# Attention queries through DRAM, a product that may be put off by a round, and new pacing of the filling work in a two-part kernel

## The chip, the cores and the metric

The kernel runs on one core of one Trainium2 chip. The metric is the device time of one execution in microseconds (us), lower is better. A core has engines that run side by side, each with its own instructions in a fixed order: PE (TensorE, matmuls and their weight loads, PEld), ACT (ScalarE), DVE (VectorE), POOL (GpSimd) and SP (SyncE). POOL, SP and ACT also issue DMAs. Engines wait for each other with semaphores.

## What is computed

Two independent computations whose outputs are put side by side, each 2048 rows x 576 columns:

```python
# A: S4 convolution, D=576 channels, N=128 states, L=2048
dt = exp(log_dt); P = exp(dt*(A_re + 1j*A_im) * l)      # l = 0..2047
K = sum_n(C * P * dt*B).real                            # one filter per channel
y = irfft(rfft(u, 2L) * rfft(K, 2L))[:L] + u * Dskip
# B: attention with 32 heads of 18 columns and one common key and value head
q = x @ wq;  k = x @ wk;  v = x @ wv
p = softmax(q . k * 18**-0.5);  out = (p @ v) @ wo
```

## The kernel before, in words

**The attention is the frame.** The queries lie in 4 chunks c of 512, the heads in 16 pairs pr per chunk, the keys in 16 blocks kb of 128. One step of the main loop's inner unit is one (pair of heads, key block): two score matmuls of PE into one PSUM tile `s` of 128 keys x 1024 (two heads x 512 queries; `scores`, L391, matmuls at L398), one exponential of ACT from `s` into an SBUF tile `P` (`exponentials`, L402, L406), and, for two such units at a time, one product v^T P (`product`, L686): four matmuls side by side at L693 that add into one PSUM tile `ops` over the 16 key blocks. Two pairs of heads, 32 units, make a head group g; 8 groups make a chunk. There are 1024 units.

**Rounds.** The loop at L704 takes NS = 3 units per round: three scores, then three exponentials, and, since one product serves two units, two products in one round and one in the next. There are 342 rounds, the last with one unit. Three PSUM slots hold the scores, so the score of a round waits until the exponential of the same place in the round before has read its slot. NP = 6 tiles hold P, so the exponential of unit i overwrites the tile of unit i - 6, which the product of that unit must have read; `while (i - NP) // 2 >= behind: product(behind)` puts the product ahead of it in the program when it is still missing.

**Fill.** Between the products and behind them, `fill` (L657) puts other work of PE into the round: q (projection of queries, `qproj` L305), op (output projection, L453 and L478), and the convolution's matmuls: kg (filter values, `kgen` L996), hu, lu, hk, lk (transforms, L1039) and iy (back transform). They share one PSUM bank `f`, so that one of them holds it until DVE has read it. All run as generators (`Stream`): the attention's `side` (queries and outputs), `prep` (normalizing), and the convolution's streams.

**The order is fixed at build time.** The programs of PE, ACT and DVE are written in the order in which the Python loop issues them. A small model, `Clock`, holds the time at which PE (`K.t`), DVE (`K.v`) and ACT (`K.a`) would be done, by constants for each operation (a product 0.96, a q group 0.43, an op group 0.50, a kg group 0.75), and the loop fills a round until the next score slot should be free. A credit limits how much fill a round may take; RATE, PACE, AHEAD, TOTAL and LAST (L37 to L41) say how fast the convolution is to move, when it counts as lagging (`lags`, L1190), how far a stream may run ahead and how much fill there is in all. POOL's and SP's orders come from a scheduler.

**Queries.** A unit (c, m) projects the queries of 7 heads (m = 4: of 4 heads) of one chunk. `qproj` leaves them in `f`; DVE or ACT makes qh, a rounded part, and ql, the rest, each in an SBUF tile with a single buffer. `queries` (L341) copies rows of them into the ring `aug`: NAUG = 9 tiles of 128 x 512, each for one pair of heads, a head at rows 0 to 54 and the other at rows 64 to 118 (18 rows qh, 18 qh, 18 ql, one row sh, a bound that is taken off so that the exponential can't overflow). These copies are DMAs from SBUF to SBUF, one per head and part, on POOL's queue (L362; L360 for the first), and one per pair for the row sh (L388). The side stream does not start a unit until the loop is within 56 steps of its due time, and waits in `queries` until the ring's tile is free (a step is two units).

**The convolution.** It runs in 12 chunks of 48 channels. `front(k)`: factors (ACT and DVE), tables (DVE), kg matmuls, the filter to DRAM (kd) and back in another layout (kt). `back(k)`: transforms of u and of the filter, the products of spectra on DVE, iy, and the store.

**The end.** The output projection of the last chunk is partly done in the loop (`outproj_part`, L478), the rest, the last head group included, in `finish` (L502), whose matmuls are named fin.

Of the kernel before, what the change touches and what calls it, by code (L numbers as in the profile page):

```python
# [36 lines left out]
RATE = 1.9  # L37
PACE = 1.8
AHEAD = 0.8
TOTAL = 330.0  # L40
LAST = 500  # L41
NAUG = 9
# [125 lines left out]
class Attention:  # L168
# [36 lines left out]
    def setup(self, tp, conv):  # L205
# [44 lines left out]
        self.aug, self.ready, self.od = {}, set(), {}  # L250
        self.outs, self.step, self.due, self.scaled = [], 0, 1 << 30, {}
        self.o_left = self.q_left = 0
        self.todo, self.busy = [], False
# [31 lines left out]
        while (0, 1) not in self.ready:  # L285
            side.advance()
# [18 lines left out]
    def qproj(self, c, m, xt):  # L305

        nc, V, K = self.nc, self.V, self.k
        m0, mn = MT[m]
        self.q_left = 10
        yield "p", K.fill, False  # L310
        ps = self.bank(CT, f"q{c}_{m}")
        for f in range(2):
            sl = slice(f * 256, f * 256 + 256)
            for k in range(5):
                matmul4(nc, ps[:, sl], self.wq[m][:, k, :], xt[:, k, sl], start=(k == 0), stop=(k == 4))
                K.pe(0.43)
                self.q_left -= 1
                if (f, k) != (1, 4):
# [22 lines left out]
    def queries(self, c, m, qh, ql, ab):  # L341

        nc, V, K = self.nc, self.V, self.k
        m0, mn = MT[m]

        last = 16 * c + ((m0 + mn) // DH - 1) // 2 - NAUG
        while self.step < 16 * (last // 2 + 1):
            yield "w", 0.0, False
        for pr in range(m0 // DH // 2, (m0 + mn) // DH // 2 + 1):
            hs = [h for h in (2 * pr, 2 * pr + 1) if m0 <= h * DH < m0 + mn]  # L350
            if 2 * pr in hs:
                self.aug[(c, pr)] = self.ring[(16 * c + pr) % NAUG]
            for row, src in ((0, qh), (18, qh), (36, ql)):
                for h in hs:
                    r, b = h * DH - m0, 64 * (h % 2) + row

                    q = nc.scalar if (c, m, pr) == (0, 0, 1) and row < 36 else nc.gpsimd
                    t = self.aug[(c, pr)]
                    if q is nc.scalar:
                        q.dma_start(t[b:b + 18, :].bitcast(F32), src[r:r + 18, :].bitcast(F32))  # L360
                    else:
                        q.dma_start(t[b:b + 18, :], src[r:r + 18, :])  # L362
# [19 lines left out]
        V.tensor_scalar(sh, un[0:2, 0:1].broadcast_to([2, CT]), -1.0, None, op0=ALU.mult)  # L382
        for h in range(m0 // DH, (m0 + mn) // DH):
            if h % 2 == 1:
                if (c, m) == (0, 0) and h < 4:
                    (nc.scalar, nc.sync)[h // 2].dma_start(self.aug[(c, h // 2)][54:119:64, :].bitcast(F32), sh.bitcast(F32))
                else:
                    nc.gpsimd.dma_start(self.aug[(c, h // 2)][54:119:64, :], sh)  # L388
                self.ready.add((c, h // 2))

    def scores(self, i, c, pr, kb, cost):  # L391

        nc, K = self.nc, self.k
        t = self.aug[(c, pr)]
        ps = self.ps_s.tile([P, 2, CT], F32, tag="s", name=f"s{c}_{pr}_{kb}")
        for j in range(2):
            r = slice(64 * j, 64 * j + 55)
            nc.tensor.matmul(ps[:, j, :], self.kaug[r, kb * P:(kb + 1) * P], t[r, :], start=True, stop=True)  # L398
        K.pe(cost, K.s[i % NS])
        return ps, K.t + 0.27  # L400
# [52 lines left out]
    def outproj(self, c):  # L453
# [4 lines left out]
        for t in range(4):  # L458
            ob = self.p1.tile([P, D], F32, tag="ob", name=f"ob{c}_{t}")
            for n in range(2):  # L460
                cs = slice(n * 288, (n + 1) * 288)
                ps = self.bank(288, f"op{c}_{t}_{n}")
                for m, (m0, mn) in enumerate(MT):
                    matmul4(nc, ps, o[:mn, m, t * P:(t + 1) * P], self.wo[:mn, m, cs], start=(m == 0), stop=(m == 4))
                    K.pe(0.5)
                    self.o_left -= 1
                    if m < 4:
# [10 lines left out]
    def outproj_part(self, c, ms, part):  # L478
# [4 lines left out]
        for t in range(4):  # L483
            for n in range(2):
# [3 lines left out]
                for m in ms:  # L488
                    matmul4(nc, ps, o[:126, m, t * P:(t + 1) * P], self.wo[:126, m, cs], start=(m == ms[0]), stop=(m == ms[-1]))
                    K.pe(0.5)  # L490
                    self.o_left -= 1
                    if m < ms[-1]:
                        yield "p", 0.0, True
                    self.late.discard((t, n, m))
# [7 lines left out]
    def finish(self, c, part, o_ps, w4, b4):  # L502
# [10 lines left out]
        def begin(t, nh, tile):  # L513

            ps[t, nh] = tile[:, :288]
            for m in range(4):
                if (t, nh, m) in self.late:
                    matmul4(nc, ps[t, nh], o[:126, m, t * P:(t + 1) * P], self.wo[:126, m, cols[nh]], start=(m == min(x[2] for x in self.late if x[:2] == (t, nh))), stop=False)
# [19 lines left out]
        while sums:  # L538
            t, nh = sums.pop(0)
            begin(t, nh, tile[t][:, nh, :])  # L540
            n0, n = n, n + sum(x[:2] == (t, nh) for x in self.late)
# [20 lines left out]
    def side(self):  # L562
# [4 lines left out]
        for c, m in units[1:]:  # L567
            due = 16 * (8 * c + (0, 1, 3, 5, 7)[m])
            self.due = due
            while self.step < due - 56:  # L570
                if self.outs:
                    yield from self.output()
                else:
                    yield "w", 0.0, False
# [3 lines left out]
            for r in self.qproj(c, m, xts[c]):  # L578
                if r[0] == "w" and self.outs:
                    yield from self.output()  # L580
                else:
                    yield r
# [7 lines left out]
    def prepare(self):  # L590

        nc = self.nc
        while True:
# [9 lines left out]
            if c == NCH - 1 and ms[0] == 0:  # L603
                self.part = self.xp.tile([P, 4, D], F32, tag="x", name="part")
                self.late = {(t, n, m) for t in range(4) for n in range(2) for m in range(4)}
# [10 lines left out]
            self.busy = False  # L616

# [17 lines left out]
    def main(self, conv, flag):  # L635
# [16 lines left out]
        def force(done):  # L652
            while not done():
                st = holder()
                (side if st is None else st).advance()

        def fill(then):  # L657
# [3 lines left out]
            while more:  # L661
                more = False
                credit = state["credit"] - (K.t - t - idle)
                urgent = self.due < self.step + 8
                for st in (prep, side, conv) if urgent else (prep, conv, side):
# [3 lines left out]
                    if st.go(self.step, max(credit - 0.3, then - K.t - 0.15, 0.3 * (st is side and side.holds and conv.lags(self.step) and credit > -1.0)), holder()):  # L669
# [10 lines left out]
            if K.t > t:  # L680

                K.t += 0.1
# [3 lines left out]
        def product(n):  # L686
# [8 lines left out]
            K.pe(0.96, done[2 * n + 1] + 0.1, self.o_free if kb == 0 else 0.0)  # L695
            state["credit"] -= 0.96
# [7 lines left out]
        for r in range(0, len(pairs), NS):  # L704
# [3 lines left out]
            for i in new:  # L708
# [3 lines left out]
                force(lambda: (c, 2 * g + j) in self.ready)  # L712
                ss[i] = self.scores(i, c, 2 * g + j, kb, 0.335 if i == r else 0.215)
            K.t += 0.11
# [10 lines left out]
            state["credit"] = min(state["credit"] + NS / 2 * (0.96 + min(max((TOTAL - state["filled"]) / max(LAST - s, 20), 0.45), 0.62 if s < 384 else 0.68)), 0.5 + 0.96)  # L725
# [4 lines left out]
            while behind < r // 2:  # L730
                fill(free() - 0.96 * (r // 2 - behind))
# [4 lines left out]
            nxt = (c, 2 * g + 3) if g < 7 else (c + 1, 1)  # L736
            if kb >= 12 and nxt[0] < NCH:
# [5 lines left out]
        while self.todo or self.busy or holder() or any(m == 0 for _, _, m in self.late):  # L743
# [92 lines left out]
class Conv:  # L836
# [159 lines left out]
    def kgen(self, k, s, ksb):  # L996
        nc, K = self.nc, self.k
        tab = K.v + 0.3
        for q in range(2):
# [9 lines left out]
            K.pe(0.75)  # L1009
# [162 lines left out]
    def go(self, step, credit, lock):  # L1172
        self.turn()
        if self.work > (step + 1) * RATE:
            return False
        for st in self.streams:
# [6 lines left out]
        for st in sorted(self.streams, key=lambda st: (not st.holds, st.work)):  # L1183
            w0 = self.k.work
# [107 lines left out]
```

## Time and profile before

| | us |
|---|---|
| median of 3 runs (lowest, highest) | 1242.33 (1239.46, 1242.68) |
| the profiled execution | 1244.62 |
| its span | 1242.8 |
| first score, last exponential (start) | 33.0, 1222.1 |
| busy: PE, ACT, DVE, POOL | 1157.0, 1045.5, 989.3, 227.6 |
| mean granted clock of TensorE, of full speed | 0.986 |

How to read what follows. A group's row is: line, engine, operation, output<-inputs, tile shapes, number of instructions, then busy time, mean time of one in ns, and the idle time of the engine just before these instructions with what ended most of it. A row of waits is: engine, tile and line <- what it waited for: us in total, times, longest. A timeline's row is: start, length, engine, line, operation, how many instructions are drawn together, and in brackets the idle time before them. Starts and lengths are in us from the start of the span. PE's matmuls overlap in its pipeline, so starts are a better measure than lengths.

### The profile page before, as it was taken

To read this page: it belongs to the slowest core of one execution; us is meant where nothing else is said; L and a number is where in the kernel's file an instruction comes from. 1 tells how busy PE (TensorE), PEld (TensorE's weight loads), DVE (VectorE), ACT (ScalarE), POOL (GpSimd) and SP (SyncE) were. 2 spreads that over 40 slices of the span, in tenths; PEclk is the share of its full clock that TensorE was granted. 3 is DMA by queue.
4 is the path that set the end of the run, shared out by engine and by line. 5 is a ranking of instruction groups with operands and counts; after the bars stand their busy time and mean duration, and the time that the engine had idled before them with its cause. 6 is when DMAs were issued, how large, how long until landed. Compare 5 with 4: busy or idle time off the path is not lost.

```text
span 1242.8 us, 32942 instructions
## 1 busy us (share of the span) xinstructions
PE 1157.0 (93%) x13762; PEld 478.2 (38%) x13762; DVE 989.3 (80%) x1607; ACT 1045.5 (84%) x1101; POOL 227.6 (18%) x451
## 2 busy tenths in 40 slices
PE   5979999899899999999999899899899899999997
PEld 1434244344334344344333343344344334334333
DVE  4656987986995997995997996897896897797753
ACT  2769989989998989888999889888888888888883
POOL 2450320222210210220412200230151110020000
PEclk9989999999999999999999999899999999899999
DMA  7621122113121112122123112112023112012111
GB/s 217 183 52 49 35 73 65 30 37 89 33 86 43 27 32 93 43 58 80 45 62 90 28 39 67 57 36 71 24 49 118 47 37 81 2 36 94 36 40 41
DMA packets 56949, 75.34 MB, mean 61 GB/s; under 512 B 19564, under 2 KB 30188, under 8 KB 56284
## 3 DMA queue, kind: packets, MB, share of 16 engines
q1 hardware_dynamic: 35788, 58.22, 14.5%
q0 software_dynamic: 20320, 14.40, 5.3%
q8 instruction: 110, 1.80, 0.6%
q10 hardware_dynamic: 688, 0.57, 0.2%
q14 instruction: 43, 0.35, 0.1%
HBM read 35.28 MB, written 22.54 MB: 47 GB/s over the span
## 4 chain that ended last, share of the span: by engine, by line
PE 64%; DVE 15%; ACT 11%; issue 4%; DMA 4%; POOL 0%; SPq 0%; ACTq 0%; DVEq 0%
PE ops L693 26%; PE s L398 18%; ACT P L406 10%; PE q L165 5%; PE op L165 4%; DVE tab L95 3%; PE kg L1007 3%; PE iy L165 2%; DVE acc L95 2%; DVE ks L95 2%; DMA xr<-xT 2%; DMA aug<-qh 2%; DVE pt L95 1%; PE hu L165 1%; PE hk L165 1%
## 5 line engine op out<-in xcount | busy, mean ns | idle before, releaser
L406 ACT ACTIVATE P<-s 128x1024 f32<-128x1024 f32 x1024 | 967.7, 1032 | 161.2 <-PE s L398 143.9
L693 PE MATMUL ops<-P,v_sb 128*32 128x512 f32 x4096 | 542.1, 603 | 7.8 <-DVE o L99 7.8
L398 PE MATMUL s<-aug,kaug 55*128 55x512 f32 x2048 | 366.3, 443 | 32.8 <-ACT P L406 30.3
L398 PEld LDWEIGHTS s<-aug,kaug 55*128 55x128 f32 x2048 | 171.2, 185 | 345.6 <-ACT P L406 307.5
L362 POOL DMA_DIRECT2D aug<-qh x252 | 126.2, 509 | 598.1 <-DVE qh L99 323.7
L693 PEld LDWEIGHTS ops<-P,v_sb 128*32 128x32 f32 x4096 | 112.2, 110 | 121.6 <-issue 78.4
L165 PE MATMUL q<-x,wq_sb 128*32 128x256 f32 (+2 forms) x1480 | 107.7, 405 | 5.2 <-DVE sck L95 3.7
L388 POOL DMA_DIRECT2D aug<-sh x62 | 35.2, 574 | 272.6 <-DVE sh L103 271.5
L165 PE MATMUL op<-wo_sb,oT 126*32 126x288 f32 (+1 forms) x1112 | 81.4, 409 | 3.2 <-DVE sck L95 1.9
L165 PEld LDWEIGHTS q<-x,wq_sb 128*32 128x32 f32 (+1 forms) x1480 | 48.9, 112 | 65.0 <-issue 38.8
L362 POOL DMA_DIRECT2D aug<-ql x128 | 63.8, 504 | 6.1 <-DMA aug<-qh 3.7
L95 DVE TENSOR_TENSOR tab<-tab,tt 128x576 f32<-128x576 f32 (+1 forms) x72 | 59.2, 822 | 1.6
L99 DVE COPY ksb<-kg 128x192 f32<-128x192 f32 x48 | 17.5, 365 | 53.3 <-PE kg L1007 52.8
L95 DVE TENSOR_TENSOR tab<-tab 128x576 f32<-128x576 f32 (+1 forms) x72 | 59.0, 820 | 1.0
L95 DVE TENSOR_TENSOR tab<-sum,r 128x576 f32<-128x576 f32 (+1 forms) x72 | 58.9, 818 | 0.0
L95 DVE TENSOR_TENSOR tab<-r,dif 128x576 f32<-128x576 f32 (+1 forms) x72 | 58.8, 817 | 0.0
L95 DVE TENSOR_TENSOR tt<-f,sum 128x576 f32<-128x576 f32 (+1 forms) x72 | 58.8, 817 | 0.0
L165 PEld LDWEIGHTS op<-wo_sb,oT 126*32 126x32 f32 (+1 forms) x1112 | 33.6, 110 | 53.5 <-issue 25.6
L1007 PEld LDWEIGHTS kg<-tab 128*32 128x32 f32 x2304 | 37.4, 112 | 32.0 <-issue 17.2
L1007 PE MATMUL kg<-tab 128*32 128x64 f32 x2304 | 42.6, 223 | 6.9 <-DVE ab L107 5.7
L95 DVE TENSOR_TENSOR acc<-acc,pt 128x1728 f32<-128x1728 f32 (+2 forms) x36 | 48.6, 1350 | 0.2
L95 DVE TENSOR_TENSOR pt<-us,ks 128x1728 f32<-128x1728 f32 (+2 forms) x36 | 48.6, 1351 | 0.0
(121 smaller groups left out, 987.1 us busy)
## 6 DMA issues: line engine op xcount, KB each, us to landing
aug<-qh POOLq DMA_DIRECT2D x252, 36.0 KB, 1.9
od<-o SPq DMA_DIRECT2D x31, 256.0 KB
aug<-ql POOLq DMA_DIRECT2D x128, 36.0 KB, 2.0
u<-u SPq DMA_DIRECT2D x12, 384.0 KB
kd<-ksb SPq DMA_DIRECT2D x12, 384.0 KB
kt<-kd SPq DMA_DIRECT2D x48, 96.0 KB
outa<-u SPq DMA_DIRECT2D x12, 384.0 KB
oT<-od SPq DMA_DIRECT2D x16, 252.0 KB
```

The source lines that it names most:

```text
L95: return self.v.tensor_tensor(out, *a, **k)
L99: return self.v.tensor_copy(out, *a, **k)
L165: nc.tensor.matmul(ps[j:e], w[:, j:e], x, start=start, stop=stop, tile_position=(0, j))
L362: q.dma_start(t[b:b + 18, :], src[r:r + 18, :])
L388: nc.gpsimd.dma_start(self.aug[(c, h // 2)][54:119:64, :], sh)
L398: nc.tensor.matmul(ps[:, j, :], self.kaug[r, kb * P:(kb + 1) * P], t[r, :], start=True, stop=True)
L406: nc.scalar.activation(pt, ps, AF.Exp, scale=SCALE)
L693: nc.tensor.matmul(o_ps[32 * j:32 * j + 32, :], self.v[:, kb, :], pts[2 * n + j // 2][:, j % 2, :], start=(kb == 0), stop=(kb == 15), tile ...
L1007: nc.tensor.matmul(ps[32 * g:32 * g + 32, d, :], t[:, :32], t[:, 32:], start=(j == 0), stop=(j == 1), tile_position=(0, 32 * g))
```

## The change

- **Queries through DRAM.** `queries` writes the parts of all heads of a unit to a DRAM tile qd of the chunk (three DMAs and one for sh, on POOL's queue); only the first two pairs still go straight into the ring. A new `fetch`, on SP's queue, reads each pair from there into a ring of 6 tiles in place of 9 (two DMAs of 55 x 512 per pair), as soon as the tile's former group is over and the queries are there.
- **Queries at any time.** The side stream no longer waits for a due time or for the ring; outputs in the queue go first, then the next unit. `late` says when the side stream may use more than its credit.
- **A product may be put off.** If the last product of a round would end more than DEFER = 0.5 after the next score slot comes free, by the model, the loop leaves it, and it comes in the next round behind the three scores, ahead of the exponential that overwrites its P tile.
- **The convolution's streams** may run further ahead of the model when they lag (up to 1.0 more), and are stopped only when they are 20 ahead.
- **Constants** of the model and of pacing, and the limits of the credit.

```diff
-RATE = 1.9
-PACE = 1.8
-AHEAD = 0.8
-TOTAL = 330.0
+RATE = 1.75
+PACE = 1.68
+AHEAD = 0.7
+TOTAL = 340.0
 LAST = 500
-NAUG = 9
+DEFER = 0.5
+NAUG = 6
+HEAD = 12
+LEFT = 0.85
...
+        self.aug = {n: self.ring[n % NAUG] for n in range(64)}
...
-                K.pe(0.43)
+                K.pe(0.465)
...
-        last = 16 * c + ((m0 + mn) // DH - 1) // 2 - NAUG
-        while self.step < 16 * (last // 2 + 1):
-            yield "w", 0.0, False
-        for pr in range(m0 // DH // 2, (m0 + mn) // DH // 2 + 1):
...
+        n0 = 4 if (c, m) == (0, 0) else 0
+        for h in range(n0):
+            t = self.aug[h // 2]
...
+        for row, src in ((0, qh), (18, qh), (36, ql)):
+            nc.gpsimd.dma_start(qd[h0 + n0:h1, row:row + 18, :], src[n0 * DH:mn, :].bitcast(F32))
...
-        sh = self.p2.tile([2, CT], F32R, tag="sh", name=f"sh{c}_{m}", bufs=1)
+        sh = self.p2.tile([8, CT], F32R, tag="sh", name=f"sh{c}_{m}", bufs=1)
...
+        nc.gpsimd.dma_start(qd[h0 + n0:h1, 54, :], sh[:h1 - h0 - n0, :].bitcast(F32))
+        self.queried = c * H + h1
+
+    def fetch(self, group):
+
+        while self.next < min(64, 2 * group + NAUG) and 2 * self.next + 2 <= self.queried:
+            c, pr = divmod(self.next, 16)
+            t = self.aug[self.next]
+            for j in range(2):
+                self.nc.sync.dma_start(t[64 * j:64 * j + 55, :].bitcast(F32), self.qd[c][2 * pr + j])
+            self.ready.add(self.next)
+            self.next += 1
...
-                    K.pe(0.5)
+                    K.pe(0.485)
...
-            while self.step < due - 56:
-                if self.outs:
-                    yield from self.output()
-                else:
-                    yield "w", 0.0, False
+            while self.outs:
+                yield from self.output()
...
+    def late(self):
+
+        s = self.step
+        if self.due < 128 and self.due - s < 2 * self.q_left + 14:
+            return True
+        return (90, 180, 270, 302)[s // 128] - self.units > LEFT * (128 * (s // 128) + (120, 120, 120, 116)[s // 128] - s)
...
-                    if st.go(self.step, max(credit - 0.3, then - K.t - 0.15, 0.3 * (st is side and side.holds and conv.lags(self.step) and credit > -1.0)), holder()):
+                    spare = credit - 0.3 if st is not side or urgent or late or side.holds else 0.0
+                    wait = then - K.t - (1.2 if st is side and not urgent and not side.holds and self.units > 0.64 * self.step + HEAD else 0.15)
+                    if st.go(self.step, max(spare, wait, 0.3 * (st is side and side.holds and conv.lags(self.step) and credit > -1.0)), holder()):
...
-                K.t += 0.1
+                K.t += 0.03
...
-            K.pe(0.96, done[2 * n + 1] + 0.1, self.o_free if kb == 0 else 0.0)
-            state["credit"] -= 0.96
+            K.pe(0.88, done[2 * n + 1] + 0.1, self.o_free if kb == 0 else 0.0)
+            state["credit"] -= 0.88
...
-            K.t += 0.11
+            K.t += 0.22
...
-            state["credit"] = min(state["credit"] + NS / 2 * (0.96 + min(max((TOTAL - state["filled"]) / max(LAST - s, 20), 0.45), 0.62 if s < 384 else 0.68)), 0.5 + 0.96)
+            state["credit"] = min(state["credit"] + NS / 2 * (0.88 + min(max((TOTAL - state["filled"]) / max(LAST - s, 20), 0.45), 0.7 if s < 384 else 0.9)), 1.2 + 0.88)
...
             while behind < r // 2:
-                fill(free() - 0.96 * (r // 2 - behind))
+                fill(free() - 0.88 * (r // 2 - behind))
+
+                if behind == r // 2 - 1 and K.t + 0.88 > free() + DEFER:
+                    break
                 product(behind)
                 behind += 1
             fill(free())
             c, g, kb, j = pairs[new[-1]]
-            nxt = (c, 2 * g + 3) if g < 7 else (c + 1, 1)
-            if kb >= 12 and nxt[0] < NCH:
+            self.group = (new[-1] + 1) // 32
+            self.fetch(self.group)
+            nxt = 16 * c + 2 * g + 3
+            if kb >= 12 and nxt < 64:
                 force(lambda: nxt in self.ready)
...
-            K.pe(0.75)
+            K.pe(0.665)
...
-        if self.work > (step + 1) * RATE:
+        lag = step * RATE - self.work
+        if lag < -20.0:
             return False
+        ahead = AHEAD + min(max(lag, 0.0) / 20.0, 1.0)
...
-            w0 = self.k.work
+            w0, st.ahead = self.k.work, ahead
```

More of the change, by code (lines that the diff above doesn't have):

```diff
@@ L249, in setup @@
         self.ubound, self.first = None, True
-        self.aug, self.ready, self.od = {}, set(), {}
+        self.aug = {n: self.ring[n % NAUG] for n in range(64)}
+        self.ready, self.od, self.qd = set(), {}, {}
+        self.next, self.queried = 2, 0
         self.outs, self.step, self.due, self.scaled = [], 0, 1 << 30, {}
-        self.o_left = self.q_left = 0
-        self.todo, self.busy = [], False
+        self.o_left = self.q_left = self.units = 0
+        self.todo, self.busy, self.group = [], False, 0
         conv.begin()
@@ L344, in queries @@
         m0, mn = MT[m]
[L346 to L362 removed]
+        h0, h1 = m0 // DH, (m0 + mn) // DH
+        if m == 0:
+            self.qd[c] = self.dr.tile([H, 55, CT], F32, tag="qd", name=f"qd{c}")
+        qd = self.qd[c]
+        n0 = 4 if (c, m) == (0, 0) else 0
+        for h in range(n0):
+            t = self.aug[h // 2]
+            for row, src in ((0, qh), (18, qh), (36, ql)):
+                b = 64 * (h % 2) + row
+                q = nc.scalar if h // 2 == 1 and row < 36 else nc.gpsimd
+                q.dma_start(t[b:b + 18, :].bitcast(F32), src[h * DH:h * DH + DH, :].bitcast(F32))
+        for row, src in ((0, qh), (18, qh), (36, ql)):
+            nc.gpsimd.dma_start(qd[h0 + n0:h1, row:row + 18, :], src[n0 * DH:mn, :].bitcast(F32))
         self.first = False
@@ L380, in queries @@
         self.ubound = un
-        sh = self.p2.tile([2, CT], F32R, tag="sh", name=f"sh{c}_{m}", bufs=1)
[L382 to L389, printed above, removed]
+        sh = self.p2.tile([8, CT], F32R, tag="sh", name=f"sh{c}_{m}", bufs=1)
+        V.tensor_scalar(sh, un[0:8, 0:1].broadcast_to([8, CT]), -1.0, None, op0=ALU.mult)
+        for pr in range(n0 // 2):
+            (nc.scalar, nc.sync)[pr].dma_start(self.aug[pr][54:119:64, :].bitcast(F32), sh[0:2, :].bitcast(F32))
+            self.ready.add(pr)
+        nc.gpsimd.dma_start(qd[h0 + n0:h1, 54, :], sh[:h1 - h0 - n0, :].bitcast(F32))
[8 more added lines that the diff above has]
+            self.next += 1
     def scores(self, i, c, pr, kb, cost):
         nc, K = self.nc, self.k
-        t = self.aug[(c, pr)]
+        t = self.aug[16 * c + pr]
         ps = self.ps_s.tile([P, 2, CT], F32, tag="s", name=f"s{c}_{pr}_{kb}")
@@ L516, in begin @@
             for m in range(4):
-                if (t, nh, m) in self.late:
-                    matmul4(nc, ps[t, nh], o[:126, m, t * P:(t + 1) * P], self.wo[:126, m, cols[nh]], start=(m == min(x[2] for x in self.late if x[:2] == (t, nh))), stop=False)
+                if (t, nh, m) in self.rest:
+                    matmul4(nc, ps[t, nh], o[:126, m, t * P:(t + 1) * P], self.wo[:126, m, cols[nh]], start=(m == min(x[2] for x in self.rest if x[:2] == (t, nh))), stop=False)
         def end(t, nh):
@@ L540, in finish @@
             begin(t, nh, tile[t][:, nh, :])
-            n0, n = n, n + sum(x[:2] == (t, nh) for x in self.late)
+            n0, n = n, n + sum(x[:2] == (t, nh) for x in self.rest)
             if n0 < 5 <= n:
@@ L577, in side @@
                 yield "v", self.k.t + 6.0, False
[L578 to L582, printed above, removed]
+            yield from self.qproj(c, m, xts[c])
         self.due = 1 << 30
@@ L604, in prepare @@
                 self.part = self.xp.tile([P, 4, D], F32, tag="x", name="part")
-                self.late = {(t, n, m) for t in range(4) for n in range(2) for m in range(4)}
+                self.rest = {(t, n, m) for t in range(4) for n in range(2) for m in range(4)}
             if ms[0] == 3:
@@ L735, in main @@
             c, g, kb, j = pairs[new[-1]]
-            nxt = (c, 2 * g + 3) if g < 7 else (c + 1, 1)
-            if kb >= 12 and nxt[0] < NCH:
+            self.group = (new[-1] + 1) // 32
+            self.fetch(self.group)
+            nxt = 16 * c + 2 * g + 3
+            if kb >= 12 and nxt < 64:
                 force(lambda: nxt in self.ready)
@@ L741, in main @@
             behind += 1
-        while self.todo or self.busy or holder() or any(m == 0 for _, _, m in self.late):
+        while self.todo or self.busy or holder() or any(m == 0 for _, _, m in self.rest):
             if self.todo or self.busy:
```

16 lines of the change are left out of this document (9 added, 7 removed).

## The prediction, made before the changed kernel ran

> **What bounds the kernel now.** I read the busy times and groups of the page first, then the waits, then short timelines in steady, crowded and stalled stretches.
>
> ```profile
> PE 1157.0 (93%) x13762; PEld 478.2 (38%) x13762; DVE 989.3 (80%) x1607; ACT 1045.5 (84%) x1101; POOL 227.6 (18%) x451
> PE 64%; DVE 15%; ACT 11%; issue 4%; DMA 4%; POOL 0%; SPq 0%; ACTq 0%; DVEq 0%
> L406 ACT ACTIVATE P<-s 128x1024 f32<-128x1024 f32 x1024 | 967.7, 1032 | 161.2 <-PE s L398 143.9
> L693 PE MATMUL ops<-P,v_sb 128*32 128x512 f32 x4096 | 542.1, 603 | 7.8 <-DVE o L99 7.8
> L398 PE MATMUL s<-aug,kaug 55*128 55x512 f32 x2048 | 366.3, 443 | 32.8 <-ACT P L406 30.3
> ```
> ```profile
> PEld s L398 <- ACT P L406: 307.5, 445, 1.5
> ACT P L406 <- PE s L398: 143.9, 224, 8.2
> DVE qh L99 <- DMA aug<-sh: 12.0, 1, 12.0
> ACT P L406 <- PE ops L693: 7.7, 5, 4.0
> PE kg L1007 <- DVE ab L107: 5.7, 1, 5.7
> ```
>
> PE and ACT wait for each other in turn: PE's score for a free score slot (445 times), ACT's exponential for a score (224 times, 143.9 us in all). So a round of three scores and three exponentials is as long as the slower of the two, and a change in their coupling moves the end directly. An exponential waits for a *product* only 5 times. How long a round is, two timelines show (start, length, engine, instruction, idle before):
>
> ```profile
> 139.90 5.61 ACT L406 ACTIVATE P<-s 128x1024 f32<-128x1024 f32 x6 [0.19 <-PE s L398]
> 141.89 0.49 PE L398 MATMUL s<-aug,kaug 55*128 55x512 f32 x2 [0.20 <-ACT P L406]
> 142.81 0.49 PE L398 MATMUL s<-aug,kaug 55*128 55x512 f32 x2 [0.42 <-ACT P L406]
> 143.23 1.92 PE L693 MATMUL ops<-P,v_sb 128*32 128x512 f32 x16
> 145.08 0.97 PE L398 MATMUL s<-aug,kaug 55*128 55x512 f32 x6
> 145.68 5.61 ACT L406 ACTIVATE P<-s 128x1024 f32<-128x1024 f32 x6 [0.18 <-PE s L398]
> ```
> ```profile
> 198.05 5.61 ACT L406 ACTIVATE P<-s 128x1024 f32<-128x1024 f32 x6 [0.66 <-PE s L398]
> 201.38 1.06 PE L693 MATMUL ops<-P,v_sb 128*32 128x512 f32 x8
> 202.27 0.83 PE L165 MATMUL hk<-kt,dft_sb 128*32 128x192 f32 x16
> 202.91 1.04 PE L693 MATMUL ops<-P,v_sb 128*32 128x512 f32 x8
> 203.89 0.96 PE L398 MATMUL s<-aug,kaug 55*128 55x512 f32 x6
> 204.49 2.85 ACT L406 ACTIVATE P<-s 128x1024 f32<-128x1024 f32 x3 [0.84 <-PE s L398]
> 204.78 0.86 PE L165 MATMUL lk<-kt,dft_sb 128*32 128x192 f32 x16
> ```
>
> Exponentials that follow each other start 0.91 apart ((2.85 - 1.03)/2), a round of three takes ACT 2.73. A product adds 1.92 - 1.06 = 0.86 to PE, the hk fill 202.91 - 202.27 = 0.64, and three scores that wait for nothing 204.78 - 203.89 = 0.89, with change-over about 1.0. Call W the products and fills of a round. Where the third score had to wait for ACT, everything behind it is late, and the round takes 1.33 + W: in the first fence six exponentials and the gap take 145.68 - 139.90 = 5.78 = 2.73 + 3.05, and 1.33 + 2 x 0.86 = 3.05; in the second 6.44 = 2.73 + 3.71, and 1.33 + 0.86 + 0.64 + 0.86 = 3.69. So the rule is max(2.73, 1.33 + W) behind a wait, else max(2.73, 1.0 + W). Over the 341 rounds of the order before it adds to 1149. The trace has 1221.46 - 33.03 = 1188.4 (first score to the last round's), so some 39 us are stalls, about 10 of them in the head, the rest places such as these:
>
> ```profile
> 33.03 1.95 PE L398 MATMUL s<-aug,kaug 55*128 55x512 f32 x6 [1.70 <-DMA aug<-qh]
> 66.51 0.69 DVE L99 CAST qh<-q 126x512 fp32r<-126x512 f32 x1 [12.04 <-DMA aug<-sh]
> 68.67 1.51 PE L1007 MATMUL kg<-tab 128*32 128x64 f32 x48 [5.67 <-DVE ab L107]
> 72.71 1.02 ACT L406 ACTIVATE P<-s 128x1024 f32<-128x1024 f32 x1 [8.19 <-PE s L398]
> 971.03 1.02 ACT L406 ACTIVATE P<-s 128x1024 f32<-128x1024 f32 x1 [3.96 <-PE ops L693]
> 1221.46 0.51 PE L398 MATMUL s<-aug,kaug 55*128 55x512 f32 x2
> 1224.13 2.61 PE L165 MATMUL fin<-wo_sb,oT 126*32 126x288 f32 x40
> ```
>
> **The change, part by part.** *Queries through DRAM.* POOL's small copies into the ring go, SP gets 124 more transfers.
>
> ```profile
> L362 POOL DMA_DIRECT2D aug<-qh x252 | 126.2, 509 | 598.1 <-DVE qh L99 323.7
> L388 POOL DMA_DIRECT2D aug<-sh x62 | 35.2, 574 | 272.6 <-DVE sh L103 271.5
> aug<-qh POOLq DMA_DIRECT2D x252, 36.0 KB, 1.9
> 47.90 5.12 SPq L303 DMA_DIRECT2D wo_sb<-wo  x5
> ```
> ```profile
> 60.00:65.00 5.00, 3.00 (x30) 0.78 (x18) 0.00 (x0) 4.17 (x5) 3.35 (x7) 1.00 0.69 171
> 65.00:70.00 5.00, 1.33 (x52) 1.36 (x56) 1.98 (x3) 0.00 (x0) 3.77 (x9) 0.73 0.18 38
> ```
>
> POOL's 442 issues (252 + 62 and 128 for ql) become some 70. POOL is busy 18%, so this alone gives nothing; but the single qh buffer came free only when POOL had issued its copies, and in the head that held DVE for 12.04, behind it PE's kernel generation for 5.67, and so ACT for 8.19. With four issues in place of some twenty the buffer is free at once: I take 8 off, between 5.67 (PE's wait alone) and 8.19 + 1.70. What is late next there are the products and fills of those rounds, which the rule above has already. On SP a fetch stands where its ring slot is free, two head groups (21 rounds of at least 2.73, 57 us) ahead of its use; behind it on SP stand loads and stores of the convolution and of the output, which wait with it. The first fetch is another matter: it stands behind the five wo loads (47.90, 5.12 long), the windows (last but one column: busy share of the DMA engines) show the transfers at 0.69 from 60 to 65 and at 0.18 behind it, and it is wanted at round 11, 33.03 + 11 x 2.73 = 63 at the earliest. Cost 0 to 3; I take 0, since fills make those rounds longer than 2.73. The sh tile has 8 rows in place of 2 and the same 512 columns, so DVE's part is as long as before. The Trainium skill, DMA: Bandwidth & Descriptors (Anatomy of one DMA — SWDGE (gpsimd) path), gives a transfer some 2 us that no size removes, mostly the receipt of the write, heaviest where it lands in HBM; the row has 1.9 for SBUF. By it the two hops in series would be an estimated 4 us or more against 1.9, which speaks against the detour; it stays behind the 57 us.
>
> *Queries at any time, new constants, longer credit.* PE's work in all stays as it is; it lies in other rounds. By the rule without any new wait the order of the changed kernel adds to 1135 in place of 1149: -14, nearly all in the last quarter, where fills now stand in rounds that had room. The middle stalls (29 of the 39) come where DVE is behind, as at 971.03; the built order spreads the convolution more evenly, and PE's longer rounds (below) give DVE time. I take -14 of them, between 0 and -29.
>
> *A product put off a round.* This decides. The changed order, read product by product, has the last product of 135 rounds behind the three scores of the next round. The six P buffers stay, so each exponential overwrites the buffer of the exponential six before it, and must wait for the product that reads that one. Before, in 170 rounds the third exponential wants the product of its own round, which by then is done. After, in 85 rounds the *second* wants the product that was put off, in 50 the *first*. Queued behind that exponential are the other exponentials of the round, and behind their ends the next scores. One place of the trace before shows such a wait:
>
> ```profile
> 82.48 1.92 PE L693 MATMUL ops<-P,v_sb 128*32 128x512 f32 x16 [0.32 <-DVE o L99]
> 83.64 1.02 ACT L406 ACTIVATE P<-s 128x1024 f32<-128x1024 f32 x1 [0.20 <-PE ops L693]
> ```
>
> From a product's start to the exponential that it releases are 83.64 - 82.48 = 1.16. Let T be the end of the last exponential of the round before. The third score can go at T + 0.18 (it needs that slot; 0.20 in the row at 141.89), the product 0.42 behind (143.23 - 142.81), the release is T + 1.76. The second exponential wants T + 0.91: stall 0.85. The first wants T: stall 1.76. So these rounds take at least 2.73 + 0.85 = 3.58 and 2.73 + 1.76 = 4.49, whatever PE has to do. Hidden is what PE's own work takes anyway: 1.0 + W is on average 3.1 in the 85 rounds (over 3.58 in 12 of them) and 3.4 in the 50 (over 4.49 in 9). Against the rule without the wait that leaves 0.36 in each of 85 = 31 and 0.84 in each of 50 = 42. And in some 80 rounds behind them PE, which now waited, starts late by 0.33: 27. Together 31 + 42 + 27 - 14 (above) = +86. Carried round by round with the same numbers, so that slack passes on, it is +79; I take +82. Bounds: -14 (all hidden) and 85 x 0.85 + 50 x 1.76 + 27 - 14 = +173 (nothing hidden); I stand near the values with the rows' own cover.
>
> *Tail.* Six more groups of the output projection are left behind the last product: five take 2.61 (1224.13), one 0.5, so +3; PE is alone there.
>
> Sum, against the profiled execution: 1244.6 + 82 - 8 - 14 + 3 = 1307.6. It stands 2.3 above the median of the runs, 1242.3, so the forecast is **1305**.
>
> **The rivals.** *The wait on P is hidden.* If the put-off product nearly always stands in rounds in which PE is the late one, the exponential comes late with or without it. For it: 224 waits of ACT for scores. Against: with six buffers and a first exponential that needs the product, the product stands between two things that ACT needs; putting it off brings the scores early and the exponentials no earlier. It decides where PE's own work passes 3.58 or 4.49, which 21 of the 135 do by my count. Then 1242.3 - 14 - 8 + 3 = 1223, with the middle stalls as they are: **faster**, or 1209 with them gone.
>
> *Fetches come late.* SP issues in order; a fetch that stands behind a store that waits for DVE reaches its pair too late. Each group of the 30 would then hold the scores for, say, the 1.9 of a landing twice: 30 x 3.8 = 114 on top, some 1400 with all of them, 1345 with a third. Against: 57 us of lead.
>
> *The change does not do what it says*: the product is hardly ever put off. The built order, with 135 such rounds, excludes it for the order itself; the effect is then that of the first rival.
>
> **How the numbers follow.** My forecast, waits on P in 135 rounds: 0.80, over 1263 (half of the +82 hidden, 1305 - 41) to 1342 (0.27 more in each of the 135 rounds, since the 1.16 is read at one place: +37). Hidden: 0.12, of which 0.11 ends below 1238.6 and 0.01 between. Late fetches: 0.08, above 1342. The range 1263 to 1342 leaves out 0.20. About 0.3% is what a measurement of this kernel can tell from no change: faster 0.11, same 0.01, slower 0.88.
>
> **What would show it.** Right: the waits of exponentials for products rise from 7.7 us, 5 times, to some 90 us in over 100; the 12.04 of DVE for qh and the 8.19 of ACT near 72 go; POOL's issues fall to some 70; no score waits for a transfer beyond the first round. Wrong: exponentials wait for scores as before and hardly for products (first rival); scores wait for fetches (second); ACT's gaps near 72 stay, or the idle time of the tail grows by more than 3.

## The result

The changed kernel takes 1323.02 us (median of 6 runs, 1317.89 to 1323.46), the kernel before 1240.78 (6 runs, 1239.46 to 1242.68): ratio 1.0648, 95% interval 1.0626 to 1.067. It is slower, by 82 us where 63 were forecast, and inside the range.

The page of the changed kernel, the lines that answer to those shown of before (busy times; the chain by engine; the groups of exponentials, products and scores, whose lines are now L417, L708 and L409):

```profile
PE 1199.6 (91%) x13762; PEld 481.7 (36%) x13762; DVE 988.8 (75%) x1601; ACT 1050.3 (80%) x1101; POOL 57.0 (4%) x97
PE 62%; ACT 19%; issue 8%; DVE 8%; DMA 2%; POOL 0%; ACTq 0%; SPq 0%; DVEq 0%
L417 ACT ACTIVATE P<-s 128x1024 f32<-128x1024 f32 x1024 | 972.3, 1030 | 231.2 <-PE ops L708 137.5
L708 PE MATMUL ops<-P,v_sb 128*32 128x512 f32 x4096 | 532.5, 609 | 5.9 <-DVE o L103 5.9
L409 PE MATMUL s<-aug,kaug 55*128 55x512 f32 x2048 | 405.9, 461 | 75.2 <-ACT P L417 65.0
```

The exponentials have not become longer (1030 ns on average in place of 1032), and their number is the same. ACT's idle time before the exponentials went from 161.2 to 231.2, and what ends it is another engine's other instruction: before it was the scores (143.9), now it is the products (137.5). In the chain of work that ended last ACT went from 11% to 19%. Of the 43 us that PE is busy longer, 40 are in the scores (405.9 against 366.3), which are the same matmuls. The waits of the changed kernel (us, times, longest):

```profile
PEld s L409 <- ACT P L417: 331.8, 557, 1.7
ACT P L417 <- PE ops L708: 137.5, 136, 3.1
ACT P L417 <- PE s L409: 88.9, 119, 10.3
```

The built order has 135 rounds in which a first or second exponential reads behind a product. In 130 of them the trace has the wait, 49 times at the first exponential (82.8 us) and 81 times at the second (51.8); the other 6 of the 136 waits are at third exponentials. Before there were 5, all at third ones. Two of the waits in a row, in the timeline (a product is eight matmul records):

```profile
58.78 1.36 PE L409 MATMUL s<-aug,kaug 55*128 55x512 f32 x6
60.07 1.92 PE L708 MATMUL ops<-P,v_sb 128*32 128x512 f32 x16
61.23 3.77 ACT L417 ACTIVATE P<-s 128x1024 f32<-128x1024 f32 x4 [1.64 <-PE ops L708]
62.78 0.94 PE L409 MATMUL s<-aug,kaug 55*128 55x512 f32 x4
64.14 0.50 PE L409 MATMUL s<-aug,kaug 55*128 55x512 f32 x2 [0.41 <-ACT P L417]
64.56 1.06 PE L708 MATMUL ops<-P,v_sb 128*32 128x512 f32 x8
65.72 2.86 ACT L417 ACTIVATE P<-s 128x1024 f32<-128x1024 f32 x3 [0.72 <-PE ops L708]
```

The three scores start at 58.78; ACT, idle from 59.59, waits 1.64 until the put-off product (60.07) has read the P tile that the first exponential overwrites: 61.23 - 60.07 = 1.16. At 64.14 the third score waits for its slot, the product follows 0.42 behind, and 65.72 - 64.56 is 1.16 again: the second exponential is 0.72 late. Over all rounds of either kind the median from the product's start to the exponential is 1.16 too.

Where the time lies, from the starts of the exponentials of rounds 0, 10, 85, 171, 256 and 341 in the traces (us between them, then their sum):

```
                          0-10   10-85  85-171  171-256  256-341    loop
before                    41.8   252.5   297.9    298.8    296.9  1187.9
changed                   37.9   276.9   322.9    322.0    301.3  1261.0
changed, 8 tiles for P    38.3   264.5   297.8    296.6    282.6  1179.8
changed, never put off    35.0   260.7   309.7    305.2    293.7  1204.3
detour alone              33.6   254.1   299.3    303.2    296.6  1186.9
```

The first exponential starts at 36.1 in place of 34.2, and what follows the last one takes 3.1 more: 1.9 + 73.1 + 3.1 = 78.1 = 1320.9 - 1242.8, the difference of the spans. The 1.9 at the start differs from run to run: with 8 tiles for P the first exponential starts at 33.9.

### The profile page after: what moved, and what is told of

Its sections match the earlier page's. It is cut to its first block, busy times and chain, and to the rows that moved or that the text cites. A ratio compares the mean times of both kernels' runs of the same rounds, so it can differ in the third digit from the quotient of the medians.

```text
span 1320.9 us, 32516 instructions
## 1 busy us (share of the span) xinstructions
PE 1199.6 (91%) x13762; PEld 481.7 (36%) x13762; DVE 988.8 (75%) x1601; ACT 1050.3 (80%) x1101; POOL 57.0 (4%) x97
## 4 chain that ended last, share of the span: by engine, by line
PE 62%; ACT 19%; issue 8%; DVE 8%; DMA 2%; POOL 0%; ACTq 0%; SPq 0%; DVEq 0%
PE ops L708 29%; ACT P L417 18%; PE s L409 18%; PE op L169 4%; PE q L169 3%; PE kg L1027 2%; PE iy L169 2%; DVE ks L99 1%; DMA xr<-xT 1%; PE hu L169 1%; DVE tab L99 1%; PE fin L169 1%; PE lk L169 1%; PE hk L169 1%; DVE sck L99 1%
## 5 line engine op out<-in xcount | busy, mean ns | idle before, releaser
L417 ACT ACTIVATE P<-s 128x1024 f32<-128x1024 f32 x1024 | 972.3, 1030 | 231.2 <-PE ops L708 137.5
L708 PE MATMUL ops<-P,v_sb 128*32 128x512 f32 x4096 | 532.5, 609 | 5.9 <-DVE o L103 5.9
L409 PE MATMUL s<-aug,kaug 55*128 55x512 f32 x2048 | 405.9, 461 | 75.2 <-ACT P L417 65.0
L409 PEld LDWEIGHTS s<-aug,kaug 55*128 55x128 f32 x2048 | 175.2, 186 | 389.8 <-ACT P L417 331.8
L708 PEld LDWEIGHTS ops<-P,v_sb 128*32 128x32 f32 x4096 | 103.6, 110 | 162.5 <-issue 136.6
L169 PE MATMUL q<-x,wq_sb 128*32 128x256 f32 (+2 forms) x1480 | 104.0, 394 | 1.3 <-DVE sck L99 1.2
L99 DVE TENSOR_TENSOR sck<-lk,sck 128x384 f32<-128x384 f32 x48 | 24.5, 552 | 44.2 <-PE lk L169 44.2
L103 DVE COPY o<-ops 128x512 f32<-128x512 f32 x31 | 21.4, 689 | 36.5 <-PE ops L708 34.4
L365 POOL DMA_DIRECT2D qd<-qh x40 | 25.3, 637 | 507.6 <-DVE qh L103 507.6
```

The lines of the kernel that those rows point to most:

```text
L99: return self.v.tensor_tensor(out, *a, **k)
L103: return self.v.tensor_copy(out, *a, **k)
L169: nc.tensor.matmul(ps[j:e], w[:, j:e], x, start=start, stop=stop, tile_position=(0, j))
L365: nc.gpsimd.dma_start(qd[h0 + n0:h1, row:row + 18, :], src[n0 * DH:mn, :].bitcast(F32))
L417: nc.scalar.activation(pt, ps, AF.Exp, scale=SCALE)
L708: nc.tensor.matmul(o_ps[32 * j:32 * j + 32, :], self.v[:, kb, :], pts[2 * n + j // 2][:, j % 2, :], start=(kb == 0), stop=(kb == 15), tile ...
```

## The experiments

Theory A: the time is lost because an exponential overwrites a P tile that the put-off product, now in its own round, has still to read. Rivals: B, the detour through DRAM and the new pacing cost the time; C, the fetches come late; D, the price belongs to the reuse of the tile and not to the place of the product.

**Never put off.**

```diff
-DEFER = 0.5
+DEFER = 1e9
```

> The changed kernel, but no product is ever put off (DEFER so large that the test never holds); its built order has 170 rounds whose third exponential reads behind a product of its own round, as before, and none with a wait of the first or second. Theory A (the put-off product holds the exponentials, the P tile being reused): the round rule adds to 1162 over the order of this kernel, the stalls of the kernels so far are 24 to 39, start and tail 59: 1245 to 1260, exponentials wait for products under 10 us. Rival B (DRAM detour and new pacing cost the time, the putting off is harmless or helps): 1310 or more, ACT's waits for scores above 150 us.

Measured: 1265.67, ratio to before 1.0189 (1.0171 to 1.0207). Exponentials wait for products 8.4 us in all, and for scores 160.7:

```profile
L417 ACT ACTIVATE P<-s 128x1024 f32<-128x1024 f32 x1024 | 966.7, 1034 | 180.1 <-PE s L409 160.7 <-DMA kaug<-keys 9.9 <-PE ops L708 8.4
```

57 of the 82 us are gone with the putting off, so B in its strong form falls. But the time is 6 above A's range: with products where they were before, the other edits cost 24. The wait for scores, 160.7 where B asked for over 150, fits that: part of the loss is B's.

**More tiles for P.** PE, ACT and DVE run the same operations in the same order as the changed kernel; only the memory behind P is larger, with the semaphore waits that follow from it, and a ring of 5 in place of 6 makes the room.

```diff
-NAUG = 6
+NAUG = 5
...
-        self.pp = ctx.enter_context(self.tc.tile_pool(name="a_p", bufs=NP))
+        self.pp = ctx.enter_context(self.tc.tile_pool(name="a_p", bufs=8))
```

> The changed kernel with 8 tiles for P in place of 6, the rule that forces a product into the program left at 6, and the ring of queries 5 tiles in place of 6 to make room: the programs of PE, ACT and DVE are the same instruction for instruction, only SP's fetches move. No exponential then wants a product that stands in its own round, but for the third in 50 rounds. Theory A: the rule without the wait adds to 1135, with 24 to 39 of stalls and 59 of start and tail 1218 to 1233: faster than before. Rival B (pacing, detour): within 10 of 1323. Rival C (fetches are late): slower than 1323, since a fetch has one group less of lead.

Measured: 1239.58, ratio 0.9972 (0.9955 to 0.999). The waits of this kernel:

```profile
PEld s L409 <- ACT P L417: 242.3, 409, 1.7
ACT P L417 <- PE s L409: 150.8, 205, 8.5
PE s L409 <- ACT P L417: 20.3, 62, 0.4
ACT P L417 <- PE ops L708: 1.5, 2, 1.1
```

The wait of 137.5 is 1.5, and 83 us are gone, without one operation moved on the three engines. This settles A: the loss is the reuse of the P tiles. C falls too: the fetches have less lead here (in the trace each pair has landed 11.6 us or more ahead of its first score, 13.8 in the changed kernel), and nothing waits for them. Against the never-put-off kernel it is 26 us faster, so under the new pacing putting off seems to be worth something where it waits for nothing; that kernel had 6 tiles and 8.4 us of waits for products, and was not run with 8. It misses A's range by 7 on the slow side: the gain that was forecast beside the wait did not come (below).

**7 tiles for P**, the ring of 6, again the same programs: `bufs=7`.

> The changed kernel with 7 tiles for P, all programs the same, the ring of 6 as well. The 50 rounds with a wait of the first exponential become rounds with a wait of the second, the 85 with a wait of the second become ones with a wait of the third, which costs nothing. Theory A: at most 50 x 0.85 = 43 and some late starts behind them above the kernel with 8 tiles, less what is hidden: 1240 to 1270, and exponentials wait for products some 50 times with a median of 0.7. Rivals B and C: 1323.

Measured: 1244.18, ratio 1.0006 (0.999 to 1.0022).

```profile
ACT P L417 <- PE s L409: 117.0, 190, 3.4
ACT P L417 <- PE ops L708: 26.5, 47, 1.9
```

One tile more turns 136 waits into 47 of 0.56 on average (the median is 0.44, where 0.7 was expected), all at second exponentials, and its loop is 3.9 longer (1183.7) than that of 8 tiles. So here the wait of a second exponential is paid for almost wholly by the shorter wait for scores behind it (117.0 against 142.3, which is 150.8 less 8.5 ahead of the very first exponential). That the wait of the first is what costs in the changed kernel follows only if its 85 rounds behave alike, which was not tested.

**The putting off alone, in the kernel before.**

```diff
+DEFER = 0.5
...
                 fill(free() - 0.96 * (r // 2 - behind))
+                if behind == r // 2 - 1 and K.t + 0.96 > free() + DEFER:
+                    break
                 product(behind)
```

> The kernel before, with one part of the change alone: a product may be put off (the test with its own model cost 0.96). Its built order has 108 rounds with a wait of the second exponential and 74 with a wait of the first. Theory A: the rule with the wait adds to 1259 in place of 1149, so with start, tail and stalls as before 1340 to 1355; exponentials wait for products some 180 times, 180 to 210 us idle. Rival B: 1200 to 1245, the waits hidden, since scores come earlier.

Measured: 1447.72, ratio 1.1656 (1.1623 to 1.1688): far outside what either theory expected. The wait is there, and the loop is 1275.5, 87.6 longer:

```profile
ACT P L407 <- PE ops L694: 186.3, 172, 3.0
```

The other 114 us come behind the loop. The last score starts at 1304.0, and then this is left (windows: PE, PEld, DVE, ACT and POOL busy, TensorE's clock, DMA share, GB/s; below them one row of PE's timeline):

```profile
1304.00:1330.00 26.00, 6.81 (x62) 1.93 (x58) 23.91 (x37) 6.67 (x6) 0.00 (x0) 0.70 0.00 1
1330.00:1360.00 30.00, 8.20 (x160) 5.57 (x160) 25.11 (x38) 0.00 (x0) 0.00 (x0) 0.50 0.00 1
1360.00:1390.00 30.00, 12.64 (x204) 6.53 (x200) 17.46 (x28) 0.00 (x0) 0.00 (x0) 0.50 0.12 40
1390.00:1420.00 30.00, 6.67 (x80) 3.33 (x79) 24.75 (x31) 0.00 (x0) 0.00 (x0) 0.50 0.00 0
```
```profile
1347.09 1.51 PE L1010 MATMUL kg<-tab 128*32 128x64 f32 x48 [33.48 <-DVE tab L96]
```

DVE still makes the tables of a convolution chunk after the attention is over. With the old pacing and the putting off the convolution does not get its share of the loop, and its rest runs alone, bound by DVE. Why was not taken apart. In the changed kernel what follows the last exponential is 3.1 longer than before and not 114; that it is the new pacing that prevents it is likely, but no run shows it by itself.

**The detour alone, in the kernel before**: `queries`, `fetch`, the ring of 6 and the calls of `fetch` as in the change; due times, constants and credit as before.

> The kernel before with one part of the change alone: the queries go through DRAM and the ring of 6 (POOL's writes, SP's fetches, no wait for the ring); due times, constants, credit as before, no product put off. Its built order adds by the round rule to 1154 in place of 1149, three groups of the output projection fewer at the end (-1.5). Theory A (the detour costs nothing in the loop, and the wait of DVE for the qh buffer in the head goes): 1233 to 1246. Rival C (the detour holds up SP's queue or the fetches): above 1255, with scores or products waiting for transfers.

Measured: 1245.85, ratio 1.0033 (1.0021 to 1.0044). Rounds 0 to 10 take 33.6 in place of 41.8: the head's wait is gone, 8.2 as the prediction said. The first exponential starts 2.2 later, and from round 10 the loop loses 7.2, of which the order (other rounds are fuller, 1154 in place of 1149 by the round rule) accounts for 5. Nothing in the loop waits for a fetch. So the detour by itself is worth nothing here, and costs 0.3%.

**The put-off product behind the second score.**

```diff
+                if i == r + 2 and behind < (r - NS) // 2:
+                    product(behind)
+                    behind += 1
                 ss[i] = self.scores(i, c, 2 * g + j, kb, 0.335 if i == r else 0.215)
```

> The changed kernel with 6 tiles for P as it is, but a product that was put off stands behind the second score of the next round in place of the third. The built order has 34 rounds in which the first exponential reads behind it and 70 in which the second does. Theory A (the price is the place: the product need not wait for the third score's slot, so it starts 0.91 earlier and releases at T + 0.8 or so in place of T + 1.76): the wait of the second exponential is gone, that of the first falls to some 0.7, 34 x 0.7 = 24 us at most in about 34 waits, total 1240 to 1265. Rival D (the price belongs to the reuse of the tile, wherever the product stands): 34 x 1.64 + 70 x 0.73 = 107 us of waits in 104 places, total 1295 to 1320.

Measured: 1271.73, ratio 1.0226 (1.0207 to 1.0245), between the two. The row of the exponentials, and two places of its timeline:

```profile
L417 ACT ACTIVATE P<-s 128x1024 f32<-128x1024 f32 x1024 | 971.1, 1033 | 184.2 <-PE s L409 115.4 <-PE ops L708 67.7
```
```profile
55.59 1.50 PE L169 MATMUL q<-x,wq_sb 128*32 128x256 f32 x24
57.03 0.73 PE L409 MATMUL s<-aug,kaug 55*128 55x512 f32 x4
57.69 1.07 PE L708 MATMUL ops<-P,v_sb 128*32 128x512 f32 x8
58.85 3.77 ACT L417 ACTIVATE P<-s 128x1024 f32<-128x1024 f32 x4 [1.57 <-PE ops L708]
60.00 1.05 PE L169 MATMUL q<-x,wq_sb 128*32 128x256 f32 x16
60.97 0.73 PE L409 MATMUL s<-aug,kaug 55*128 55x512 f32 x4
61.63 1.07 PE L708 MATMUL ops<-P,v_sb 128*32 128x512 f32 x8
62.80 1.94 ACT L417 ACTIVATE P<-s 128x1024 f32<-128x1024 f32 x2 [0.17 <-PE ops L708]
```

The second exponential's wait falls from 0.72 to 0.17, as the place would have it; the first's is still 1.57 there. PE comes to these scores straight from its fills (q from 55.59, the scores at 57.03 without a wait for a slot), so it is PE and not the slot that sets when the product starts, and standing ahead of the third score helps little. Over all rounds it is alike: 43 waits at second exponentials are 8.1 us, 34 at first ones 52.4. So A holds for the second exponentials and D for the first; both are too simple. How much of the 51 us gained against the changed kernel is the place's is open, since this order also has fewer such rounds (104 in place of 135).

**Versions that keep the putting off and take the wait away.** The rule that forces products set to 8 as well (`NP = 8`, `NAUG = 5`):

> The changed kernel with 8 tiles for P, the ring of 5, and the rule that forces a product set to 8 as well, so that a product that was put off may stand behind the fills of its round. Round rule 1131 in place of 1135, three groups fewer at the end than the kernel with 8 tiles. Theory A: 1230 to 1240, no exponential waits for a product. Rival: the forced place kept PE busy at the right time, 1245 or more.

Measured: 1238.88, ratio 0.9974 (0.9958 to 0.9991), inside A's range, but not told apart from the 1239.58 with the rule at 6. Exponentials still wait for products 3 times, 5.3 us. Then with `LEFT = 0.6`:

> The changed kernel with 8 tiles for P, the rule at 8, the ring of 5, and LEFT = 0.6 in place of 0.85, so that the side stream may exceed its credit earlier. The built order has 7 rounds with over 4.2 us of products and fills (8 with LEFT at 0.85), 4 rounds in which the one bank of the fills changes hands more than once (9), and two groups of the output projection fewer at the end (-1). If the stalls that are left come where fills hand the bank over behind DVE, 1228 to 1237, below the 1238.88 with LEFT at 0.85; if they have nothing to do with the order of the fills, 1237 to 1241.

Measured: 1233.98, ratio 0.9934 (0.9914 to 0.9954): the fastest, 0.66% below the kernel before and 89 us below the changed one. The time fits the forecast that stalls fall with fewer hand-overs of the bank, but the traces do not bear it out: in the profiled executions (1237.65 and 1238.2) exponentials wait for scores 152.2 us, with LEFT at 0.85 they wait 145.4, and the loop is 2.7 longer. What makes it faster stays open.

## Why the prediction was right, and where its sizes were off

The step that decided was right in place, kind and nearly in count: of the 135 rounds forecast 130 show the wait; the price's parts, 0.42 and 1.16, are the same in the changed kernel's timeline; with the tiles free the wait goes and 83 us with it. The idle time is larger than forecast, 137.5 us in place of some 90.

Its size splits into classes when the changed kernel and the one with 8 tiles, which run the same programs, are set side by side (ACT's time between the starts of exponentials above 0.91, added over the rounds of a class, a round going from the last exponential of the round before to its own last):

```
rounds that wait with the   count   forecast   measured
first exponential              50        +42      +72.6
second exponential             85        +31      +18.3
neither (late starts)         205        +27       -9.7
sum                                     +100      +81.2
```

The sum is firm: 81 where 96 (82 + 14) was forecast. Which of the three terms was mis-sized can't be read from it, since the split depends on where a round is cut: from first score to first score, as the prediction's rule counts, the same two traces give +19.9, +48.7 and +13.2.

What is seen directly is this. Ahead of the first exponential of the 50 rounds ACT is idle 1.69 on average (84.4 us), where I had 1.76. PE is not late there: in 44 of the 50 rounds the first score starts more than 0.4 before the last exponential of the round before has ended. So the wait is not hidden in its own round, as I had it for half of it. What it hides is the lateness of the next round: 48 of the 50 are followed by a round in which the second exponential waits, and in these the time ahead of the first exponentials, above 0.91 each, adds to 44.5 with 8 tiles and to 5.1 in the changed kernel. The wait of the second exponentials puts 40.5 in its place.

That the total lies inside the range is in part luck: the wait came out 15 below its forecast, and the terms beside it, together -33 by the forecast (-8, -14 of stalls, -14 of the order, +3), came out at -3, 30 above.

The terms beside it came out worse:

- The last quarter gains 14.3 with 8 tiles (282.6 against 296.9): the -14 that the order's rule had there.
- The head gives 3.5 to 3.9 (rounds 0 to 10), not 8. The wait of DVE for qh is gone, in place of 12.04 stands a wait for the projection itself, 7.5. The detour alone gave 8.2; with the rest of the change q groups fill those early rounds, and in the changed kernel exponentials wait for products in them. The first exponential starts 1.9 later.
- The middle stalls do not go. Rounds 10 to 85 take 12.0 *more* with 8 tiles, though by the rule they should be even. Its trace has seven waits of exponentials above 1.5 us there, 14.7 in all, where the kernel before has two, 4.0 in all; the shorter ones add to the same (18.4 and 18.5). The longest of the seven, in that kernel's timeline:

```profile
227.89 1.07 PE L708 MATMUL ops<-P,v_sb 128*32 128x512 f32 x8
228.88 1.45 DVE L99 TENSOR_TENSOR r<-r,m 128x1248 f32<-128x1248 f32 x1
230.25 0.68 DVE L103 COPY o<-ops 128x512 f32<-128x512 f32 x1
230.98 1.93 PE L708 MATMUL ops<-P,v_sb 128*32 128x512 f32 x8 [2.02 <-DVE o L103]
233.75 1.94 ACT L417 ACTIVATE P<-s 128x1024 f32<-128x1024 f32 x2 [3.59 <-PE s L409]
```

The head group ends at 228.9; the copy of its result, which frees the PSUM tile for the next, stands on DVE behind an operation of the convolution, and PE idles 2.02, and ACT 3.59. Another of the seven (2.45, ending at 318.68) has PE waiting for DVE too; ahead of three (82.53, 185.43 and 261.50; 5.35 in all) PE has no wait but is full of q and products, and ahead of one (207.00, 1.61) it waits for the transfer kt<-kd. I had reasoned that DVE's spare time would absorb the stalls. At two of these places the order of DVE's queue counts, at three how the fills lie. -14 was forecast, +9.7 measured (all rounds from 10 to 256).
- The tail: 3.1, forecast 3.
- POOL's issues fall from 442 to 88, forecast some 70: four for each of 20 units, and 8 straight into the ring.

Together, against the span: +81.2, -14.3, -3.5, +9.7, +1.9 and +3.1 are 78.1.

The first rival (the wait is hidden) is out by the wait's 137.5; so is "the change does not do what it says". The second (late fetches) is out: beyond the first score (3.6, put down to a DRAM write of the head) no score waits for a transfer. Its prices were added loosely: 1305 + 114 is 1419, and with a third 1343, where the prediction has some 1400 and 1345. The queries' way through DRAM takes 5.1 us from issue to landing for the first hop and 2.4 (median, 1.8 to 2.7) for the second. The first pair fetched has only 13.8 from landing to use, not 57 of lead, which is still enough:

```profile
aug<-qd SPq DMA_DIRECT2D x124, 110.0 KB
qd<-qh POOLq DMA_DIRECT2D x30, 252.0 KB, 5.1
qd<-sh POOLq DMA_DIRECT2D x15, 14.0 KB, 1.9
```

The Trainium skill, DMA: Bandwidth & Descriptors (Anatomy of one DMA — SWDGE (gpsimd) path), has a fixed part of some 2 us per transfer, heaviest for writes to HBM. The trace agrees with the 2 us, but does not show that DRAM is the heavier target: 14 KB of sh land there in 1.9, as 36 KB did in SBUF before, and the 5.1 belongs to 252 KB.

## What to carry to other kernels

When work is moved later, look up which buffer it still holds: a consumer that is put off turns a free buffer into a wait of the producer, and the producer here is one of the two engines that bound the loop. Trace each reuse (this exponential, that tile, the product between them) in the built order and count the rounds; 130 of the 135 rounds so found show the wait. One buffer more in place of the wait is worth trying first, since it changes no program: 7 tiles took back 79 of the 82 us. Average slack of an engine does not hide a queue's order: an operation that others wait for must be looked at in its place.

## What the runs showed of the hardware

Work that is left over behind the loop runs slower there: in the tail of the kernel before with the putting off alone, PE was busy 7 to 13 us in windows of 30, the granted clock was 0.50, and 48 kg matmuls took 1.51 us, where the same group takes 0.85 (median) over that run. The pace was set by DVE all the same, busy 17 to 25 of 30. The Trainium skill, TensorE: Matmul & The Clock Gate (Part 1: The HAM clock gate), has half the clock for a PE that was idle a few microseconds before; the windows agree, 0.50 from 1330 to 1420.
